# Key-value sums in quarters of the array, queries' A and B in halves, and the first weight slice loaded between the two pieces of the first batch's values

## The chip, the cores and the metric

One core of one Trainium2 chip runs the whole program. The metric is device time in microseconds (us), from the first to the last instruction of one execution, as the median of three executions. Engines are named as in the profile: PE (TensorE matmuls), PEld (its weight loads), DVE (VectorE), ACT (ScalarE), POOL (GpSimd), SP (SyncE, which issues nearly all DMAs).

## The reference, cut to what matters

An attention without softmax feeds a gated linear unit. `phi` is the outer product of two small projections of a vector of 32 numbers, so it has 64 features.

```python
batch, n_heads, seq, head_dim = (4, 4, 1088, 32);  r = 8
def phi(x):
    a = einsum('rd,bhsd->bhsr', S1, x)          # "A"
    b = einsum('rd,bhsd->bhsr', S2, x)          # "B"
    return einsum('bhsi,bhsj->bhsij', a, b)     # 64 features
kv  = einsum('bhsf,bhsd->bhfd', phi(k), v);  z = sum(phi(k), axis=2)
x   = einsum('bhsf,bhfd->bhsd', phi(q), kv) / (einsum('bhsf,bhf->bhs', phi(q), z) + 1e-6)
# n_tokens 4352, d_model 128, d_ff 1536
xn  = x / sqrt(mean(x*x) + 1e-6) * rms_g
out = (silu(xn @ w_gate) * (xn @ w_val)) @ w_out
```

## The kernel before, in words

The 4352 tokens are cut into nine chunks (eight of 512, one of 256). For each batch of keys (`kside`), PE makes A and B (line 489), DVE or POOL the outer product `phi` (L511), and PE the sums over tokens `kv`. For batch 0 these sums are 36 matmuls of 64 x 34 (L541: nine tiles of tokens by four heads); two heads share a group of 64 output rows each. For the first two chunks of queries, `qphi` makes A and B with the tokens as the stationary side (L582, 128 tokens a matmul), the outer product `phn` on DVE (L591), four transposes (L601, which write `phiq` through a copy, L615). From chunk 2 on it takes A and B to DRAM (`far`, L631), reads them back spread over partitions (`at` L638, `bt` L645) and multiplies them on POOL or DVE (L651). `qside` then multiplies `phiq` by `kv` (`nmm`, L669), divides (L727, L728, L720), takes the mean square (L734, L744), its root on POOL (L765), scales (`xn`, L768 on DVE or L788 on ACT), transposes (L772), and splits the result into `x_hi` (L795, ACT) and `x_lo` (L775, DVE).

The weights come as 64-bit words in twelve slices (`weights(j)`, L391). Each is turned into f32 by an Abs on ACT or DVE (L338 or L318 first), then L318, L323, L328 and L332 on DVE, and then split into `w_hi` (L243, ACT, or L244, DVE) and `w_lo` (L250, POOL, or L251, DVE). A slot (chunk c, slice j) is a gate and a value product of three matmuls each (L830), a Silu on ACT (L837), the product `h` on DVE (L841) and the output matmuls (L848 in f32 for the first twelve slots, later L861 with `h_hi`, L243, and `h_lo`, L250 or L251). Chunks 0 and 1 go through slices 0 to 5 first, then through 6 to 11.

Nothing of the order is written out by hand: every step is a task with a cost, a key and its ways (which engine may do it, with a penalty), and `Plan.run` lists them greedily by these. The order it finds is then fixed, one queue for each engine, and an instruction that waits holds up all that stands behind it on its engine. PE is kept busy in gaps by `keep_warm`, matmuls of zeros (L300). The numbers at the head of the file are such penalties and keys; DMAs are issued by SP in the order that the plan finds.

Of the kernel before, what the change touches and what calls it, by code (L numbers as in the profile page):

```python
# [21 lines left out]
F = R * R  # L22
NT = B * S
P = 128
# [3 lines left out]
KT = 9  # L28
SP = KT * P
HALF = 64  # L30
# [28 lines left out]
HOP = 160  # L59
COPY_DVE = 600  # L60
REST_DVE = 500
ABS_ACT = -300
NATURAL = 2
PHIS = 2
PUT_DVE = 100
PHIQ_DVE = 600
CUT = 6
TURNED = (1, 2, 3)
HBUFS = 3
GAIN = -28.5  # L70
EXACT = 2
EARLY = 12
SPLIT = 6
HEAD = 2
K1 = -41,9,10,-28.2
VT1 = (-15, -14, -13)
SBD = (1,)
AB2 = (-21, -20, -19)
KVO = ()
Q0 = (-61, -57, -56)  # L80
LATER = 12
KLATE = 2500
DLAT = 2400
CHAIN = -52
WAIT = 150
WKEY = {0: -50, 1: -43}
XN_ACT = 150
Q0L = -97.8
Q1 = (8, 6, 5)
Q1L = -25  # L90
KO = (20, 18, 16)
QO = (20, 10, 6)


class Buf:
# [115 lines left out]
def attention_then_glu(ctx, tc, kT, v, qT, sw, w, gain, out):  # L211
    nc = tc.nc
# [9 lines left out]
    def ps(name, bufs):  # L222
        return plan.buf(psum, [P, 512], F32, name, bufs)

    def pe(ns, key, emit, reads, writes, part=False):
        plan.add({"pe": (ns, emit, 0, part)}, key, reads, writes)
# [52 lines left out]
    for b in range(B):  # L279
        t = const.tile([P, 2, 2 * (D + 1)], F32, name=f"kv{b}")  # L280
# [6 lines left out]
    sblk_t = const.tile([P, NB], F32, name="s_t")  # L287
# [99 lines left out]
    def weights(j, key, early):  # L387
        raw, tmp = sb("w_raw", [P, 3 * P, 2], RAWS, U32), sb("w_tmp", [P, 3 * P], TBUFS)
        load(
            P * 3 * P * 8, early,  # L390
            lambda: nc.sync.dma_start(  # L391
                out=raw().rearrange("p n c -> p (n c)"), in_=w.bitcast(U32)[:, 6 * P * j:6 * P * (j + 1)]
            ), [raw],
        )
        to_f32(3 * P, key, lambda: w_f[:, j].rearrange("p a n -> p (a n)"), raw, tmp, [raw], [tmp], [("w", j)])
        split(j, slice(0, 2), key)

    abs_of, ahead = {}, {}
# [65 lines left out]
    def kside(b, keys, early):  # L464
        first = b == 0
        kab, kphi, key = keys
        kt, vt, kv = sb("kt", [P, SP], 2), sb("vt", [P, KT, H, VA], 2), kvs[b]
# [11 lines left out]
        piece = [next(g for g, (_, e) in enumerate(pieces) if hi <= e) for _, hi in groups]  # L479
        abs_ = [sb("ab", [P, 2, 3, H, R], 3) for _ in groups]  # L480
        phis = [sb("phi", [P, 3, H * F], 4) for _ in groups]
# [20 lines left out]
        for i, (lo, hi) in enumerate(groups):  # L502
            g, m, ts = piece[i], hi - lo, slice(0, hi - lo)
            ab_ps, o = (banks[i], 0) if first else (banks[i // 2], i % 2 * 3 * HALF)
# [30 lines left out]
        for i, (lo, hi) in enumerate(groups):  # L535
            def kvmm(lo=lo, hi=hi, phi=phis[i]):
                kvv = acc()[:, :2 * VA].rearrange("p (a x) -> p a x", x=VA)
                for t in range(lo, hi):
                    for h in range(H):
                        rows = slice((h % 2) * F, (h % 2 + 1) * F)  # L540
                        nc.tensor.matmul(  # L541
                            out=kvv[rows, h // 2, :], lhsT=phi()[:, t - lo, h * F:(h + 1) * F], rhs=vt()[:, t, h, :],
                            start=(t == 0 and h < 2), stop=(t == KT - 1), skip_group_check=True,
                        )

            pe(275 * (hi - lo), key, kvmm, [(phis[i], i), (vt, piece[i])], [acc], True)
        for hh in range(2):
            def put(eng, rows=slice(hh * F, (hh + 1) * F), xs=slice(hh * (D + 1), (hh + 1) * (D + 1))):
                kvv = acc()[:, :2 * VA].rearrange("p (a x) -> p a x", x=VA)
# [15 lines left out]
    def qphi(c, kab):  # L565
        n = CHUNKS[c]
        nt = n // P
        first = c == 0
        key0 = kab
        q, phi = phiqs[c]  # L570
        if c < NATURAL:

            ab, pn = sb("abq", [P, 4, H, R], 1), sb("phn", [P, 4, H * F], 1)
            for u in range(0, nt, 2):
                kab = key0 + (1 if first and u else 0)
                us = slice(u, u + 2)
                ab_ps = ps("att", 3)
                tr = ps(("g_ps", "v_ps")[u // 2], 2) if first else ps("att", 3)

                def abmm(u=u, ab_ps=ab_ps):  # L580
                    for t in range(2):
                        nc.tensor.matmul(  # L582
                            out=ab_ps()[:, t * HALF:(t + 1) * HALF], lhsT=q()[:, (u + t) * P:(u + t + 1) * P], rhs=sblk_t,
                            start=True, stop=True,
                        )

                def near(ab_ps=ab_ps):
                    return ab_ps()[:, :2 * HALF].rearrange("p (th c r) -> p th c r", c=2, r=R)

                def outer(us=us, near=near):  # L590
                    nc.vector.tensor_tensor(  # L591
                        out=pn()[:, us].rearrange("p t (h i j) -> p (t h) i j", h=H, i=R),
                        in0=near()[:, :, 0, :].unsqueeze(3).to_broadcast([P, 2 * H, R, R]),
                        in1=ab()[:, us].rearrange("p t h r -> p (t h) r").unsqueeze(2).to_broadcast([P, 2 * H, R, R]),
                        op=ALU.mult,
                    )

                def turn(u=u, tr=tr):
                    for p in range(2):
                        for t in range(2):  # L600
                            nc.tensor.transpose(  # L601
                                out=tr()[:, (2 * p + t) * P:(2 * p + t + 1) * P], in_=pn()[:, u + t, p * P:(p + 1) * P], identity=ident
                            )

                pe(440, kab, abmm, [q, "sblk"], [ab_ps])
                act(
                    HALF, kab, lambda us=us, near=near: nc.scalar.copy(
                        out=ab()[:, us].rearrange("p t h r -> p (t h) r"), in_=near()[:, :, 1, :]
                    ), [ab_ps], [(ab, u)],
                )  # L610
                dve(2 * 268, kab, outer, [(ab, u), ab_ps], [(pn, u)])
                pe(440, kab, turn, [(pn, u)], [tr])

                def put(eng, u=u, tr=tr):
                    eng(out=phi()[:, :, u * P:(u + 2) * P], in_=tr().rearrange("p (a s) -> p a s", a=2))  # L615

                plan.add({
                    "act": (512 * 0.835 + 144, lambda put=put: put(nc.scalar.copy), 0),
                    "dve": (512 * 1.04 + 140, lambda put=put: put(nc.vector.tensor_copy), PUT_DVE),
                }, kab, [tr], [(phi, u)])  # L620
        else:


            m = n // 2
            ab, at, bt = sb("abt", [P, 256], 2), sb("at", [P, 2, 512], 1), sb("bt", [P, 2, 512], 1)
            ab_ps = abs_of[c]
            act(m, kab, lambda: nc.scalar.copy(out=ab()[:, :m], in_=ab_ps()[:, :m]), [ab_ps], [ab])
            far = plan.buf(dram, [2 * H * R, 512], F32, "far", 2)
            for t in range(2):
                load(  # L630
                    H * R * n * 4, kab, lambda t=t: nc.sync.dma_start(  # L631
                        out=far()[:, t * m:(t + 1) * m], in_=ab()[t * HALF:(t + 1) * HALF, :m]
                    ), [(far, t)], [ab],
                )
            for p in range(2):
                rows = slice(2 * p * R, 2 * (p + 1) * R)
                load(
                    P * n * 8, kab, lambda p=p, rows=rows: nc.sync.dma_start(  # L638
                        out=at()[:, p, :n], in_=far()[rows, :n].unsqueeze(1).to_broadcast([2 * R, R, n])
                    ), [(at, p)], [(far, 0), (far, 1)],  # L640
                )
                for o in range(2):
                    rows = slice((H + 2 * p + o) * R, (H + 2 * p + o + 1) * R)
                    load(
                        F * n * 8, kab, lambda p=p, o=o, rows=rows: nc.sync.dma_start(  # L645
                            out=bt()[o * F:(o + 1) * F, p, :n], in_=far()[rows, :n].unsqueeze(0).to_broadcast([R, R, n])
                        ), [(bt, p, o)], [(far, 0), (far, 1)],
                    )

                def times(eng, p=p):  # L650
                    eng.tensor_tensor(out=phi()[:, p, :n], in0=at()[:, p, :n], in1=bt()[:, p, :n], op=ALU.mult)  # L651

                plan.add({
                    "pool": (n * 2.1 + 150, lambda times=times: times(nc.gpsimd), 0),
                    "dve": (n * 1.04 + 140, lambda times=times: times(nc.vector), PHIQ_DVE, True),
                }, kab, [(at, p), (bt, p, 0), (bt, p, 1)], [(phi, "p", p)])
# [35 lines left out]
    def qside(c, keys, also=None):  # L692
# [3 lines left out]
        phi = phiqs[c][1]  # L696
# [58 lines left out]
        for u, wd in ((0, 2), (2, 2)) if first else ((0, nt),):  # L755
# [2 lines left out]
            xt = ps("att", 3)  # L758
            if first and not u:

                ahead[1] = [ps("att", 3) for _ in range(2)]
            ids = list(range(u, u + wd, 2))

            def root(us=us):
# [137 lines left out]
    qphi(0, Q0[0])  # L902
    qside(0, Q0[1:])
    for j in range(NJ):
        weights(j, WKEY.get(j, slots.index((0, j)) - 4), -30 + 2 * j)
    for j in range(NJ):
        split(j, slice(2, 3), max(EARLY, slots.index((0, j))) + j % CUT - SPLIT if (0, j) in slots else 0)
    t1 = begin[1]
# [72 lines left out]
```

## Time and profile before

| | |
|---|---|
| median of 3 executions | 266.39 us (266.28 to 266.45) |
| profiled execution, its own time | 267.68 us |
| its span, first to last instruction | 265.9 us |
| PE busy | 260.0 us, 98% |
| DVE, ACT, POOL busy | 189.6, 153.0, 66.8 us |
| DMA | 22.11 MB, 83 GB/s over the span |

Busy time is time in which an engine has an instruction in it; the clock that PE was granted is shown in tenths of full speed. A row of a timeline has the start, the duration, the engine, the line and the tiles (out<-in), the shape, how many instructions it merges, and in brackets how long the engine sat idle before it and what ended that. A f32 matmul that is no transpose leaves two records, so "x48" at L541 are 24 matmuls.

### The profile page before, as it was taken

The page shows a single profiled execution, that of the slowest core. Times are in us where ns is not written, and L with a number is a line of the kernel's source. Part 1 is how long each engine was busy: PE and PEld are TensorE (multiplying, and loading weights), DVE is VectorE, ACT ScalarE, POOL GpSimd, SP SyncE. Part 2 cuts the span into 40 slices and gives each one's busy share as a digit, 9 for nine tenths or more (in the row PEclk, how much of TensorE's full clock was granted, in tenths as well). Part 3 has the DMA queues.
Part 4 walks back from the last instruction along what each step waited for, and adds up shares of the span by engine and source line. Part 5 has one row for each costly group of instructions (what it writes and reads, how often), then busy time and mean ns, then how long its engine had stood idle before and what let it go on. Part 6 is the DMA issues. An engine that isn't in the chain of part 4 may idle for free.

```text
span 265.9 us, 5111 instructions
## 1 busy us (share of the span) xinstructions
PE 260.0 (98%) x1913; PEld 206.8 (78%) x1913; DVE 189.6 (71%) x375; ACT 153.0 (58%) x319; POOL 66.8 (25%) x83
## 2 busy tenths in 40 slices
PE   8989999999989999999999999999999999999995
PEld 6877676678867887878887877788878888788894
DVE  3789997787956886677566796677667566766532
ACT  4377673484744644565556554665656565665662
POOL 5053661265060150002700220012200700100262
PEclk9999999999999999999999999999999999999999
DMA  6999801721511430035002500034002100100010
GB/s 201 362 382 313 264 2 32 218 64 62 148 49 53 125 85 2 1 101 145 13 2 79 140 20 4 0 101 118 1 0 76 55 0 0 42 1 0 0 42 21
DMA packets 13097, 22.11 MB, mean 83 GB/s; under 512 B 1680, under 2 KB 5904, under 8 KB 13072
## 3 DMA queue, kind: packets, MB, share of 16 engines
q1 hardware_dynamic: 12928, 21.72, 26.4%
q8 instruction: 15, 0.25, 0.4%
q14 instruction: 10, 0.08, 0.1%
q10 hardware_dynamic: 144, 0.07, 0.1%
HBM read 18.69 MB, written 3.08 MB: 82 GB/s over the span
## 4 chain that ended last, share of the span: by engine, by line
PE 84%; DMA 8%; SPq 3%; POOL 1%; ACT 1%; issue 1%; DVE 1%; POOLq 0%
PE g_ps L830 25%; PE v_ps L830 25%; PE o_ps L861 21%; DMA w_raw<-w 4%; PE o_ps L848 4%; PE att L669 3%; DMA bt<-far 2%; DMA far<-abt 2%; PE att L414 1%; PE att L685 1%; PE att L772 1%; PE att L489 1%; SPq L645 1%; POOL h_lo L250 1%; POOL phiq L651 0%
## 5 line engine op out<-in xcount | busy, mean ns | idle before, releaser
L841 DVE TENSOR_TENSOR h<-v_ps,s 128x512 f32<-128x512 f32 (+2 forms) x109 | 71.1, 655 | 25.1 <-PE v_ps L830 13.7
L243 ACT CAST h_hi<-h 128x512 fp32r<-128x512 f32 (+1 forms) x91 | 54.2, 596 | 49.2 <-DVE h L841 49.0
L837 ACT ACTIVATE s<-g_ps 128x512 f32<-128x512 f32 (+1 forms) x108 | 62.1, 575 | 25.1 <-PE g_ps L830 22.5
L251 DVE TENSOR_TENSOR h_lo<-h,h_hi 128x512 fp32r<-128x512 f32 x76 | 53.3, 704 | 32.2 <-ACT h_hi L243 31.1
L830 PE MATMUL g_ps<-x_hi,w_hi 128*128 128x512 f32 (+1 forms) x110 | 45.8, 416 | 0.0
L830 PE MATMUL v_ps<-x_hi,w_hi 128*128 128x512 f32 (+1 forms) x110 | 42.0, 382 | 0.0
L830 PE MATMUL g_ps<-x_hi,w_lo 128*128 128x512 f32 (+1 forms) x110 | 41.9, 381 | 0.0
L830 PE MATMUL v_ps<-x_hi,w_lo 128*128 128x512 f32 (+1 forms) x110 | 41.6, 378 | 0.0
L830 PE MATMUL v_ps<-x_lo,w_hi 128*128 128x512 f32 (+1 forms) x110 | 41.5, 378 | 0.0
L830 PE MATMUL g_ps<-x_lo,w_hi 128*128 128x512 f32 (+1 forms) x110 | 41.5, 378 | 0.0
L861 PE MATMUL o_ps<-h_lo,w_hi 128*128 128x512 f32 (+1 forms) x94 | 36.0, 383 | 0.9 <-POOL h_lo L250 0.9
L765 POOL TENSOR_TENSOR rstd<-ms,mhalf 128x4 f32<-128x4 f32 (+1 forms) x10 | 9.2, 924 | 108.8 <-DVE ms L781 108.3
L861 PE MATMUL o_ps<-h_hi,w_lo 128*128 128x512 f32 (+1 forms) x94 | 36.1, 384 | 0.0
L861 PE MATMUL o_ps<-h_hi,w_hi 128*128 128x512 f32 (+1 forms) x94 | 35.9, 382 | 0.0
L830 PEld LDWEIGHTS g_ps<-x_hi,w_hi 128*128 128x128 f32 x110 | 20.7, 188 | 6.3 <-issue 1.5
L651 POOL TENSOR_TENSOR phiq<-at,bt 128x512 f32<-128x512 f32 (+1 forms) x14 | 18.0, 1285 | 29.3 <-DMA bt<-far 22.1
L250 POOL TENSOR_TENSOR h_lo<-h,h_hi 128x256 fp32r<-128x256 f32 (+1 forms) x18 | 18.2, 1018 | 27.4 <-ACT h_hi L243 27.3
L830 PEld LDWEIGHTS v_ps<-x_hi,w_hi 128*128 128x128 f32 x110 | 20.7, 188 | 4.8 <-DVE h L841 0.5
L830 PEld LDWEIGHTS g_ps<-x_hi,w_lo 128*128 128x128 f32 x110 | 20.7, 188 | 4.8 <-issue 1.2
L250 POOL TENSOR_TENSOR w_lo<-w_f,w_hi 128x256 fp32r<-128x256 f32 (+1 forms) x24 | 17.8, 755 | 26.3 <-ACT w_hi L243 26.2
L830 PEld LDWEIGHTS g_ps<-x_lo,w_hi 128*128 128x128 f32 x110 | 20.8, 189 | 4.2
L830 PEld LDWEIGHTS v_ps<-x_lo,w_hi 128*128 128x128 f32 x110 | 20.7, 188 | 4.1
(107 smaller groups left out, 302.7 us busy)
## 6 DMA issues: line engine op xcount, KB each, us to landing
w_raw<-w SPq DMA_DIRECT2D x12, 384.0 KB
at<-far SPq DMA_DIRECT2D x12, 256.0 KB
bt<-far SPq DMA_DIRECT2D x24, 128.0 KB
q<-qT SPq DMA_DIRECT2D x8, 256.0 KB
outT<-o_sb SPq DMA_DIRECT2D x8, 256.0 KB
vt<-v SPq DMA_DIRECT2D x9, 204.0 KB
kt<-kT SPq DMA_DIRECT2D x9, 192.0 KB
far<-abt SPq DMA_DIRECT2D x12, 64.0 KB
```

The costliest lines, as they stand in the source:

```text
L243: "act": (n * 0.835 + 172, lambda: nc.scalar.copy(out=out(), in_=in_()), 0),
L250: "pool": (n * 2.1 + 150, lambda: nc.gpsimd.tensor_tensor(out=out(), in0=in_(), in1=hi(), op=ALU.subtract), 0),
L251: "dve": (n * 1.04 + 140, lambda: nc.vector.tensor_tensor(out=out(), in0=in_(), in1=hi(), op=ALU.subtract), penalty, True),
L414: nc.tensor.matmul(out=acc()[rows, :F], lhsT=vt()[:, t, h, :D], rhs=phis[t // 3]()[:, t % 3, h * F:(h + 1) * F], start=(t == 0), stop=(t = ...
L651: eng.tensor_tensor(out=phi()[:, p, :n], in0=at()[:, p, :n], in1=bt()[:, p, :n], op=ALU.mult)
L669: nc.tensor.matmul(out=nv[hf * HALF:(hf + 1) * HALF, t, p, :], lhsT=phiqs[c][1]()[:, p, l0:l0 + HALF], rhs=kvs[(STARTS[c] + l0) // S][:, p ...
L765: nc.gpsimd.tensor_tensor(out=rstd()[:, us, 0], in0=ms()[:, us], in1=mhalf[:, us], op=ALU.pow)
L830: nc.tensor.matmul(out=acc()[:, cs], lhsT=wt[:, j, i3, :], rhs=x()[:, cs], start=(i == 0), stop=(i == 2))
L837: act(n, t + 0.3, lambda: nc.scalar.activation(out=s()[:, :n], in_=gps()[:, :n], func=AF.Silu), cols(gps, whole[0]), [s])
L841: lambda cs=cs: nc.vector.tensor_tensor(out=h()[:, cs], in0=vps()[:, cs], in1=s()[:, cs], op=ALU.mult),
L848: lambda cs=cs: nc.tensor.matmul(out=o_ps()[:, cs], lhsT=w_f[:, j, 2], rhs=h()[:, cs], start=first, stop=last and cs.stop == n),
L861: nc.tensor.matmul(out=o_ps()[:, :n], lhsT=wt[:, j, 2, :], rhs=x()[:, :n], start=first and i == 0, stop=last and i == 2,)
```

## The change

Three edits in the code, and new values for the plan's numbers. The sums of batch 0 (L541) are made by 72 matmuls of 32 x 34 instead of 36 of 64 x 34, and the plan is told 130 ns a tile of tokens instead of 275. A and B of the first two chunks' queries (L582) are made by matmuls of 64 tokens, twice as many, which the plan counts among the forms that use a part of the array. The first weight slice has a load key of its own, `W0L`, that lies between those of the two pieces of the first batch's values. The A and B of batch 1's keys write to banks of `g_ps` and `v_ps` instead of `att`. The other numbers move penalties (an outer product `phiq` on DVE costs 300 more than on POOL instead of 600; the copy of the transposes on DVE 600 instead of 100; Abs on DVE 500 instead of 300; `xn` on ACT nothing instead of 150) and keys; three slots instead of two go in halves (`HEAD`).

```diff
-ABS_ACT = -300
+ABS_ACT = -500
-PUT_DVE = 100
-PHIQ_DVE = 600
+PUT_DVE = 600
+PHIQ_DVE = 300
-SPLIT = 6
-HEAD = 2
-K1 = -41,9,10,-28.2
+SPLIT = 8
+HEAD = 3
+K1 = (-45, 3, 15, -29.5)
-AB2 = (-21, -20, -19)
+AB2 = (4, -20, 4)
-CHAIN = -52
-WAIT = 150
+CHAIN = -47
+WAIT = 100
-XN_ACT = 150
+XN_ACT = 0
+W0L = -97.3
...
                     for h in range(H):
-                        rows = slice((h % 2) * F, (h % 2 + 1) * F)
-                        nc.tensor.matmul(
-                            out=kvv[rows, h // 2, :], lhsT=phi()[:, t - lo, h * F:(h + 1) * F], rhs=vt()[:, t, h, :],
-                            start=(t == 0 and h < 2), stop=(t == KT - 1), skip_group_check=True,
-                        )
-
-            pe(275 * (hi - lo), key, kvmm, [(phis[i], i), (vt, piece[i])], [acc], True)
+                        for x in range(0, F, F // 2):
+                            r0 = h % 2 * F + x
+                            nc.tensor.matmul(
+                                out=kvv[r0:r0 + F // 2, h // 2, :], lhsT=phi()[:, t - lo, h * F + x:h * F + x + F // 2],
+                                rhs=vt()[:, t, h, :], start=(t == 0 and h < 2), stop=(t == KT - 1), skip_group_check=True,
+                            )
+
+            pe(130 * (hi - lo), key, kvmm, [(phis[i], i), (vt, piece[i])], [acc], True)
...
                     for t in range(2):
-                        nc.tensor.matmul(
-                            out=ab_ps()[:, t * HALF:(t + 1) * HALF], lhsT=q()[:, (u + t) * P:(u + t + 1) * P], rhs=sblk_t,
-                            start=True, stop=True,
-                        )
+                        for hf in range(2):
+                            s0 = (u + t) * P + hf * HALF
+                            nc.tensor.matmul(
+                                out=ab_ps()[hf * HALF:(hf + 1) * HALF, t * HALF:(t + 1) * HALF], lhsT=q()[:, s0:s0 + HALF],
+                                rhs=sblk_t, start=True, stop=True,
+                            )
...
-                ahead[1] = [ps("att", 3) for _ in range(2)]
+                ahead[1] = [ps(name, 2) for name in ("g_ps", "v_ps")]
...
-        weights(j, WKEY.get(j, slots.index((0, j)) - 4), -30 + 2 * j)
+        weights(j, WKEY.get(j, slots.index((0, j)) - 4), W0L if j == 0 else -30 + 2 * j)
```

What the plan makes of it, at three places. Lines of the changed kernel stand up to five higher than before (L489 is L490, L541 is L544, L582 is L587, L601 is L606, L651 is L656, L669 is L674, L772 is L777, L830 is L835, L841 is L846).

SP, the first loads. `kt`, `vt` and `q` are the keys, values and queries, `w_raw` a weight slice. Before:

```order
L472 DMA kt<-kT 128x512
L472 DMA kt<-kT 128x640
L562 DMA q<-qT 128x512
L475 DMA vt<-v 128x544
L475 DMA vt<-v 128x680
L391 DMA w_raw<-w 128x768
L899 DMA gain_t<-gain 128x1
L472 DMA kt<-kT 128x384 x3
```

and now:

```order
L473 DMA kt<-kT 128x512
L473 DMA kt<-kT 128x640
L565 DMA q<-qT 128x512
L476 DMA vt<-v 128x544
L392 DMA w_raw<-w 128x768
L476 DMA vt<-v 128x680
L473 DMA kt<-kT 128x384 x3
L904 DMA gain_t<-gain 128x1
```

The first weight slice stands ahead of the second piece of the values; the rest of this piece is the same.

PE, from the sums of batch 0 to the first gate matmul of chunk 0. `phn` and `xn` are transposed, `kv_83` is batch 0's sums. Before:

```order
L582 MATMUL att<-s_t,q 128x64 x4
L541 MATMUL o_ps<-vt,phi 64x34 x24
L601 MATMUL g_ps<-ident,phn 128x128 x4
L541 MATMUL o_ps<-vt,phi 64x34 x12
L601 MATMUL v_ps<-ident,phn 128x128 x4
L669 MATMUL att<-kv_83,phiq 64x66 x16
L300 MATMUL att<-const-float32-0.0 1x128 x11
L772 MATMUL att<-ident,xn 128x128 x2
L489 MATMUL att<-s_t,kt 64x64 x18
L772 MATMUL att<-ident,xn 128x128 x2
L830 MATMUL g_ps<-x_hi,w_hi 128x256
```

and now:

```order
L587 MATMUL att<-s_t,q 64x64 x8
L544 MATMUL o_ps<-vt,phi 32x34 x32
L606 MATMUL g_ps<-ident,phn 128x128 x4
L301 MATMUL att<-const-float32-0.0 1x128
L544 MATMUL o_ps<-vt,phi 32x34 x40
L606 MATMUL v_ps<-ident,phn 128x128 x4
L674 MATMUL att<-kv_83,phiq 64x66 x16
L490 MATMUL g_ps<-s_t,kt 64x64 x12
L490 MATMUL v_ps<-s_t,kt 64x64 x6
L777 MATMUL att<-ident,xn 128x128 x2
L301 MATMUL att<-const-float32-0.0 1x128 x2
L835 MATMUL g_ps<-x_hi,w_hi 128x256
```

Batch 1's A and B (18 matmuls) moved ahead of the first transposes, the eleven matmuls of zeros became three, and the second pair of transposes went behind the gate products.

DVE, after chunk 0's sum of its two output parts (`o_sb`). `phiq` is the outer product of a later chunk's queries, `h` and `h_lo` belong to slots. Before:

```order
L892 TENSOR_TENSOR o_sb<-o_ps,part 128x512
L841 TENSOR_TENSOR h<-v_ps,s 128x512
L775 SCALAR_TENSOR_TENSOR x_lo<-att,gain_t,x_hi 128x512
L841 TENSOR_TENSOR h<-v_ps,s 128x512
L251 TENSOR_TENSOR h_lo<-h,h_hi 128x512 x2
L841 TENSOR_TENSOR h<-v_ps,s 128x512 x2
L251 TENSOR_TENSOR h_lo<-h,h_hi 128x512
```

and now:

```order
L897 TENSOR_TENSOR o_sb<-o_ps,part 128x512
L846 TENSOR_TENSOR h<-v_ps,s 128x512
L780 SCALAR_TENSOR_TENSOR x_lo<-att,gain_t,x_hi 128x512
L846 TENSOR_TENSOR h<-v_ps,s 128x512
L656 TENSOR_TENSOR phiq<-at,bt 128x512
L252 TENSOR_TENSOR h_lo<-h,h_hi 128x512 x2
L846 TENSOR_TENSOR h<-v_ps,s 128x512 x2
L656 TENSOR_TENSOR phiq<-at,bt 128x512
L252 TENSOR_TENSOR h_lo<-h,h_hi 128x512 x2
```

Both `phiq` products of this chunk stand on DVE now. Of the fourteen in all, fourteen stood on POOL before; now eight stand on DVE and six on POOL.

## Rows read from the trace of the kernel before

**Rows 1.** The page: busy time of the engines, and two lines of the span in 40 equal slices (busy tenths of PE, and the clock granted to it).

```profile
PE 260.0 (98%) x1913; PEld 206.8 (78%) x1913; DVE 189.6 (71%) x375; ACT 153.0 (58%) x319; POOL 66.8 (25%) x83
...
PE   8989999999989999999999999999999999999995
...
PEclk9999999999999999999999999999999999999999
```

**Rows 2.** Waits of PE within the program: the line that waited, what it waited for, us in total, times, the longest.

```profile
PE o_ps L861 <- POOL h_lo L250: 0.9, 1, 0.9
PE att L772 <- DVE xn L768: 0.8, 1, 0.8
...
PE o_ps L848 <- DVE h L841: 0.2, 1, 0.2
```

**Rows 3.** Timeline of PE, 7 to 19 us.

```profile
7.66 1.67 PE L541 MATMUL o_ps<-vt,phi 128*64 128x34 f32 x48
...
9.85 0.89 PE L541 MATMUL o_ps<-vt,phi 128*64 128x34 f32 x24
10.68 0.65 PE L601 MATMUL v_ps<-ident,phn 128*128 128x128 f32 x4
11.38 1.32 PE L669 MATMUL att<-kv,phiq 128*64 128x66 f32 x32
12.62 2.60 PE L300 MATMUL att<-const-float32-0.0 128*1 128x128 f32 x22
16.04 0.41 PE L772 MATMUL att<-ident,xn 128*128 128x128 f32 x2 [0.81 <-DVE xn L768]
16.38 1.27 PE L489 MATMUL att<-s_t,kt 128*64 128x64 f32 x36
17.63 0.52 PE L772 MATMUL att<-ident,xn 128*128 128x128 f32 x2
17.90 0.36 PE L830 MATMUL g_ps<-x_hi,w_hi 128*128 128x256 f32 x1
...
18.22 0.29 PE L830 MATMUL g_ps<-x_lo,w_hi 128*128 128x256 f32 x1
18.34 0.56 PE L582 MATMUL att<-s_t,q 128*128 128x64 f32 x4
18.71 0.36 PE L830 MATMUL v_ps<-x_hi,w_hi 128*128 128x256 f32 x1
```

**Rows 4.** Timeline of DVE between the copy of the first transposes and the first `x_lo`.

```profile
11.35 0.36 DVE L323 TENSOR_SCALAR w_tmp<-w_tmp 128x384 uint32<-128x384 uint32 x1
...
12.34 0.56 DVE L332 SCALAR_TENSOR_TENSOR w_f<-w_raw,w_tmp 128x384 uint32<-128x384 uint32 x1
12.93 0.17 DVE L727 TENSOR_SCALAR den<-att 128x8 f32<-128x8 f32 x1
...
15.47 0.42 DVE L768 TENSOR_TENSOR xn<-x,rstd 128x256 f32<-128x256 f32 x1
...
16.99 0.49 DVE L775 SCALAR_TENSOR_TENSOR x_lo<-att,gain_t,x_hi 128x256 fp32r<-128x256 f32 x1 [0.52 <-ACT x_hi L795]
```

**Rows 5.** Timelines of SP (the issue that waited for `vt`'s first piece, and the one that waited for its second), and of ACT (the first work on slice 0, which waited for its load).

```profile
7.54 0.33 SPq L391 DMA_DIRECT2D w_raw<-w  x1
...
8.56 0.33 SPq L562 DMA_DIRECT2D q<-qT  x1
...
9.52 0.55 ACT L338 ACTIVATE w_tmp<-w_raw 128x384 f32<-128x384 f32 x1 [1.71 <-DMA w_raw<-w]
```

**Rows 6.** Timeline of PE at the sums of batch 1: matmuls of 32 columns of the array with 32 (L410) and 64 (L414) moving columns, and the one behind them.

```profile
43.29 0.34 PE L410 MATMUL att<-ab 128*32 128x32 f32 x17
43.44 0.26 PE L414 MATMUL att<-phi,vt 128*32 128x64 f32 x3
...
44.60 0.66 PE L685 MATMUL att<-q,sab 128*64 128x128 f32 x8
```

**Rows 7.** Timelines of ACT and POOL near the first gate: `x_hi`, the `xn` of the second half of the chunk, and the root before it.

```profile
16.48 0.47 ACT L795 ACTIVATE x_hi<-att,gain_t 128x256 fp32r<-128x256 f32 x1 [0.47 <-PE att L772]
17.07 0.70 ACT L788 ACTIVATE xn<-x,rstd 128x128 f32<-128x128 f32 x2
...
16.30 0.74 POOL L765 TENSOR_TENSOR rstd<-ms,mhalf 128x2 f32<-128x2 f32 x1 [0.99 <-DVE ms L781]
```

**Rows 8.** Timelines of POOL, SP and PE at chunk 3's queries: the two products of `phiq` and the `h_lo` behind them; the two stores to `far` and the loads behind them; the PE matmul that waited.

```profile
73.25 1.29 POOL L651 TENSOR_TENSOR phiq<-at,bt 128x512 f32<-128x512 f32 x1 [6.50 <-PE v_ps L830]
75.72 1.30 POOL L651 TENSOR_TENSOR phiq<-at,bt 128x512 f32<-128x512 f32 x1 [1.17 <-DMA bt<-far]
76.98 1.74 POOL L250 TENSOR_TENSOR h_lo<-h,h_hi 128x512 fp32r<-128x512 f32 x1
...
61.97 1.14 SPq L631 DMA_DIRECT2D far<-abt  x2
...
66.92 0.56 SPq L638 DMA_DIRECT2D at<-far  x1
...
78.77 0.51 PE L861 MATMUL o_ps<-h_lo,w_hi 128*128 128x512 f32 x1 [0.85 <-POOL h_lo L250]
```

**Rows 9.** DVE there, and what POOL's `phiq` products waited for over the whole span (us, times).

```profile
71.27 0.69 DVE L841 TENSOR_TENSOR h<-v_ps,s 128x512 f32<-128x512 f32 x1
...
  DMA bt<-far: 22.1, 9
```

More of the change, by code (lines that the diff above doesn't have):

```diff
@@ L83 @@
 DLAT = 2400
-CHAIN = -52
-WAIT = 150
+CHAIN = -47
+WAIT = 100
 WKEY = {0: -50, 1: -43}
-XN_ACT = 150
+XN_ACT = 0
 Q0L = -97.8
-Q1 = (8, 6, 5)
-Q1L = -25
+Q1 = (8, 5, 4)
+Q1L = -23
+W0L = -97.3
 KO = (20, 18, 16)
-QO = (20, 10, 6)
+QO = (18, 10, 7)
 class Buf:
@@ L603, in turn @@
                             )
-                pe(440, kab, abmm, [q, "sblk"], [ab_ps])
+                pe(250, kab, abmm, [q, "sblk"], [ab_ps], True)
                 act(
```

## The prediction, made blind

> **What bounds the kernel now.** I read the page first: PE is busy 98% of a span of 265.9 us, no other engine over 78%, and its granted clock is full in every slice [rows 1]. So the time is PE's, and the list of PE's waits shows what of it is not work: 0.8 us for `xn` near the start, 0.2 and 0.9 later [rows 2]. Third, PE's timeline: between the last product with batch 0's sums and the first transposes of `xn` stand 2.60 us of matmuls of zeros and the wait of 0.81, which is 3.4 us from 12.62 to 16.04 in which PE computes nothing; from 16.04 on it works without a break worth naming except at 22.6 and 78.77 [rows 2, 3, 8]. Hence only three things can shorten the span: the first gate product coming earlier than 17.90, the wait at 78.77 going away, or PE getting less to do after 17.90. DVE's timeline says why the gap is there: the denominators of the first two token tiles could be read when the first half of the L669 matmuls is done, at 11.38 + 0.62 = 12.00, but `den` starts at 12.93, right behind the conversion of weight slice 0, which DVE finishes at 12.90 [rows 3, 4]. That conversion begins when the slice lands, at about 9.5; the two pieces of the values land at about 7.54 and 8.56, where SP's waits for them end [rows 5].
>
> **The change, part by part.** All times are those of the profiled execution. Its own time is 267.68 us, 1.8 over its span, and the median of the runs is 266.39; I carry a difference in the span over to the median one to one.
>
> *Loads.* Slice 0 and the second piece of the values change places. The slice took 0.95 us of the queue (8.56 to 9.5), the piece 1.02 (7.54 to 8.56) [rows 5]: now the slice is there at 8.5 and the values at 9.5. Slice 0 gains 1.0 us, the sums of batch 0 must wait 1.0 us longer for their second piece.
>
> *Sums in quarters.* The last twelve matmuls of L541 took from 9.85 to 10.68, 69 ns each [rows 3]; 36 of them are 2.5 us. The new form, 32 columns of the array with 34 moving, isn't in this trace. From below: nine matmuls of L410 with 32 moving columns took from 43.29 to 43.44, 17 ns each; from above 36 of L414 with 64 took from 43.44 to 44.60, 32 ns each [rows 6]. By columns 34 lies next to the first, I take 20 (72 in 1.4 us; bounds 1.2 and 2.3). [...]
>
> On the path 40 of the 72 stand behind the values' landing: start at 9.6 (as 7.66 follows 7.54 [rows 3, 5]), 0.8 us, end at 10.4 instead of 10.68 (bounds 10.3 and 10.9). So the better matmuls just pay for the later load, with 0.3 us over.
>
> *The way to the first gate.* The L669 matmuls began 0.70 us after the sums' end; now that is 11.1, and their first half is done at 11.7 [rows 3]. Slice 0's conversion ended at 12.90 [rows 4]; 1.0 earlier is 11.9, and DVE loses a copy of the transposes and one of the sums to ACT but gets a cast. I let `den` start at 11.8, 1.1 us earlier. From `den` to the start of `xn` were 2.54 us [rows 4]; `xn` is on ACT now, 0.70 [rows 7] for 0.42, but isn't behind a weight operation: its end moves from 15.89 to 14.9. From there to the end of `x_lo` (17.48) were 1.59 us [rows 4]; ACT now has the second half's squares in that stretch, for which I add 0.1: `x_lo` is done at 16.6, and the third gate matmul, which stood at 18.22 [rows 3], starts there, 1.6 us earlier. Batch 1's A and B (16.38 to 17.63 [rows 3]) cost nothing, since they lie in the old gap; were their keys late they would push the gate, by up to 1.25. The second pair of transposes (17.63 to 17.90) is still to come: net gain there 1.3 us.
>
> *What PE then lacks.* PE runs ahead of its supply. The second half of `x` needs squares, root (0.74), `xn` (0.70, among weight casts on ACT), transposes, `x_hi` (0.47) and `x_lo` (0.49) [rows 4, 7], each a little over 0.1 from the next: about 3 us after the first `xn` at 14.9 plus what ACT and POOL do in between, so 18.5 to 19.0. Until then PE has four groups of three matmuls (0.36 each [rows 3]) and one AB of 0.3, some 1.8 us from 16.6 on: 0.1 to 0.6 short. Slice 1's `w_lo` waits behind the root on POOL, and chunk 1's `phn` and `phiq` copies come up earlier, too. I charge 0.8 us for these waits (bounds 0.3 and 1.3). The head gains 0.5 us (bounds 0 and 1.0).
>
> *Halves for A and B.* Two matmuls of L582 took 0.37 us (18.34 to 18.71); four of 64 at L489's rate of 69 ns (18 from 16.38 to 17.63) are 0.28 [rows 3]. Twice 0.09, less a change of form: nothing, with 0.2 as the bound. The pair at the start is hidden behind the values' first piece. The third slot in halves is the same columns: nothing, bound 0.2 either way.
>
> *The wait at 78.77.* PE stood 0.85 us for an `h_lo` on POOL, which started at 76.98 behind two `phiq` products that had waited for `bt` [rows 8]. Both products go to DVE, so that `h_lo` isn't behind them: 0.85 gained, if DVE finds its operands there.
>
> Sum: 0.5 + 0.85 = 1.35 us off. 266.39 - 1.35 = 265.0.
>
> **The rivals.** *The wait at chunk 3 moves to DVE.* DVE gets to its first `phiq` after the `h` of 71.27, at 71.96 [rows 9]; POOL's could start at 73.25 [rows 8]. With the same transfers DVE stands 1.3 us, and two `h_lo` and all later `h` stand behind it. For it: the far store took from 61.97 to beyond 66.9 there [rows 8], and nothing in the change shortens that. Against: the transfer's delay belongs to that moment, and DVE had air around it. PE then pays about what it paid, 0.85: 265.9.
>
> *DVE's waits for transfers, at several chunks: slower.* Eight of the fourteen products stand on DVE now. On POOL nine of them waited 22.1 us in total for `bt` [rows 9], 2.5 us each, and it cost PE little, since POOL is busy 25%; DVE is busy 71% [rows 1] and makes every `h`. At 0.85 us a place it takes three places to outweigh the gain and make the kernel measurably slower: 265.0 + 2.55 = 267.6. Against: the products stand later in DVE's queue than POOL's did.
>
> [...]
>
> *No waits after the first gate.* If PE's supply keeps up, the head gains 1.2: 264.3. *No gain in the head*, if the values land later than the swap says: 265.5.
>
> **How the numbers follow.** Forecast 0.48 (its own range 264.4 to 265.6), wait moved to DVE 0.20, several DVE waits 0.12, dear quarters 0.04, no waits after the gate 0.10, no gain in the head 0.06. A measurement can tell about 0.2%, 0.53 us: below 265.86 is faster, above 266.92 slower. Faster: 0.45 of the forecast's 0.48, 0.08 of the second, both last cases but 0.01: 0.68. Slower: 0.09 of the DVE waits, 0.04 and 0.01: 0.14. Same: 0.18. The range 264.0 to 266.8 leaves out some 0.03 below and 0.13 above.
>
> **What would show it.** Slice 0's Abs starts near 8.6; L544's second part starts near 9.6 and takes 0.8 us; `den` stands near 11.8; the first gate's third matmul near 16.6; PE's list of waits gets several of 0.1 to 0.6 us before 24; the wait for POOL's `h_lo` is gone. It is wrong if DVE's idle time is put down to `bt`, if L544 takes over 30 ns a matmul, or if PE, with no zeros to work on, is granted half the clock somewhere before 20 us.

## The result: slower, and the profile after

The changed kernel takes 268.56 us (median of 4, 267.94 to 269.12) against 266.40 for the kernel before: a ratio of 1.0081, 95% interval 1.0055 to 1.0108. Measured again beside other kernels it took 268.67 (6 executions) against 266.90, a ratio of 1.0068 (1.0044 to 1.0093). I had forecast 265.0, faster, with a range up to 266.8. The sign was wrong, and the time lies above the range.

The page of the changed kernel, which answers to [rows 1]: busy times, and the two lines of the span in 40 slices.

```profile
PE 258.3 (97%) x1991; PEld 205.5 (77%) x1991; DVE 192.4 (72%) x377; ACT 155.8 (58%) x330; POOL 55.7 (21%) x77
...
PE   8589999999999999999999999999999999999995
...
PEclk9979999999999999999999999999999999999999
...
q8 instruction: 15, 0.25, 0.4%
```

The last line is a DMA queue: packets, MB, share of the 16 engines. Two digits say where to look: in the second slice (6.7 to 13.4 us) PE is busy half of the time, and in the third (13.4 to 20.0) it was granted 0.7 of its clock. Everything behind looks as before. The list of PE's waits answers to [rows 2] (line that waited, on what, us in total, times, longest):

```profile
PE att L674 <- issue: 2.4, 1, 2.4
PE o_ps L544 <- DMA vt<-v: 0.8, 2, 0.5
...
PE att L777 <- ACT xn L793: 0.7, 1, 0.7
PE g_ps L835 <- DVE x_lo L780: 0.4, 1, 0.4
```

The `h_lo` of POOL is gone from it, as I had said; the kernel before, profiled again, lacks it too (see "The wait at 78.77"). In its place stands a wait of 2.4 us that the profile puts down to "issue", that is, to nothing it can see. PE's timeline around it answers to [rows 3]:

```profile
9.52 0.90 PE L544 MATMUL o_ps<-vt,phi 128*32 128x34 f32 x80 [0.47 <-DMA vt<-v]
10.35 0.66 PE L606 MATMUL v_ps<-ident,phn 128*128 128x128 f32 x4
13.38 2.03 PE L674 MATMUL att<-kv,phiq 128*64 128x66 f32 x32 [2.37 <-issue]
15.19 1.47 PE L490 MATMUL g_ps<-s_t,kt 128*64 128x64 f32 x24
16.47 0.54 PE L490 MATMUL v_ps<-s_t,kt 128*64 128x64 f32 x12
17.66 0.62 PE L777 MATMUL att<-ident,xn 128*128 128x128 f32 x2 [0.65 <-ACT xn L793]
...
19.41 0.39 PE L835 MATMUL g_ps<-x_lo,w_hi 128*128 128x256 f32 x1
```

L674 stands at 13.38, where I had it at 11.1. Its last operand was there long before: ACT's copy of `phiq` is this row, done at 11.63, and `kv` was done at 10.94.

```profile
11.04 0.59 ACT L620 COPY phiq<-v_ps 128x512 f32<-128x512 f32 x1
```

What PE did then it did slowly: the 32 records of L674 took 1.8 us, 1.2 before [rows 3]. The same span by stretches (length, PE busy and its instructions, granted clock, DMA share, GB/s) shows a clock of 0.5 right behind the 2.1 us in which PE had nothing to do:

```profile
11.00:13.10 2.10, 0.01 (x1) 1.00 1.03 402
13.10:16.50 3.40, 3.12 (x58) 0.50 1.04 414
16.50:20.00 3.50, 2.75 (x29) 1.00 0.52 170
```

So the third gate product came at 19.41 and not at 18.22 [rows 3], 1.2 us later instead of 1.6 earlier.

### The profile page after: what moved, and what is told of

The parts are those of the page before. It is cut to its first block, busy times and chain, and to the rows that moved or that the text cites. A ratio compares the mean times of both kernels' runs of the same rounds, so it can differ in the third digit from the quotient of the medians.

```text
span 267.2 us, 5268 instructions
## 1 busy us (share of the span) xinstructions
PE 258.3 (97%) x1991; PEld 205.5 (77%) x1991; DVE 192.4 (72%) x377; ACT 155.8 (58%) x330; POOL 55.7 (21%) x77
## 4 chain that ended last, share of the span: by engine, by line
PE 88%; DVE 4%; DMA 2%; ACT 2%; issue 1%; SPq 1%; POOL 0%; DVEq 0%
PE g_ps L835 26%; PE v_ps L835 26%; PE o_ps L866 23%; PE o_ps L853 4%; PE att L674 3%; DMA vt<-v 2%; PE att L777 1%; PE att L690 1%; PE att L490 1%; PE att L415 1%; DVE phi L512 1%; DVE w_tmp L319 1%; DVE phn L596 0%; DVE w_f L333 0%; ACT phiq L620 0%
## 5 line engine op out<-in xcount | busy, mean ns | idle before, releaser
L846 DVE TENSOR_TENSOR h<-v_ps,s 128x512 f32<-128x512 f32 (+2 forms) x109 | 71.0, 654 | 25.4 <-PE v_ps L835 14.6
L835 PE MATMUL g_ps<-x_hi,w_hi 128*128 128x512 f32 (+1 forms) x111 | 47.2, 425 | 0.1
L835 PE MATMUL g_ps<-x_lo,w_hi 128*128 128x512 f32 (+1 forms) x111 | 41.8, 377 | 0.4 <-DVE x_lo L780 0.4
L835 PE MATMUL v_ps<-x_hi,w_hi 128*128 128x512 f32 (+1 forms) x111 | 42.0, 378 | 0.1
L835 PE MATMUL v_ps<-x_lo,w_hi 128*128 128x512 f32 (+1 forms) x111 | 41.8, 376 | 0.0
L835 PE MATMUL g_ps<-x_hi,w_lo 128*128 128x512 f32 (+1 forms) x111 | 41.7, 376 | 0.0
L835 PE MATMUL v_ps<-x_hi,w_lo 128*128 128x512 f32 (+1 forms) x111 | 41.5, 374 | 0.0
L251 POOL TENSOR_TENSOR h_lo<-h,h_hi 128x512 fp32r<-128x512 f32 (+1 forms) x20 | 20.6, 1034 | 64.5 <-ACT h_hi L244 64.5
L835 PEld LDWEIGHTS g_ps<-x_hi,w_hi 128*128 128x128 f32 x111 | 20.9, 188 | 7.2 <-issue 1.7
L835 PEld LDWEIGHTS g_ps<-x_hi,w_lo 128*128 128x128 f32 x111 | 20.9, 188 | 5.8 <-issue 1.7
L835 PEld LDWEIGHTS g_ps<-x_lo,w_hi 128*128 128x128 f32 x111 | 20.9, 188 | 4.9 <-DVE x_lo L780 0.9
L835 PEld LDWEIGHTS v_ps<-x_hi,w_hi 128*128 128x128 f32 x111 | 20.8, 188 | 4.4 <-DVE h L846 0.2
L835 PEld LDWEIGHTS v_ps<-x_lo,w_hi 128*128 128x128 f32 x111 | 20.8, 188 | 4.0
L835 PEld LDWEIGHTS v_ps<-x_hi,w_lo 128*128 128x128 f32 x111 | 20.9, 188 | 4.0
L251 POOL TENSOR_TENSOR w_lo<-w_f,w_hi 128x128 fp32r<-128x128 f32 (+1 forms) x24 | 15.5, 664 | 25.4 <-ACT w_hi L244 21.0
```

The costliest lines, as they stand in the source:

```text
L251: "pool": (n * 2.1 + 150, lambda: nc.gpsimd.tensor_tensor(out=out(), in0=in_(), in1=hi(), op=ALU.subtract), 0),
L835: nc.tensor.matmul(out=acc()[:, cs], lhsT=wt[:, j, i3, :], rhs=x()[:, cs], start=(i == 0), stop=(i == 2))
L846: lambda cs=cs: nc.vector.tensor_tensor(out=h()[:, cs], in0=vps()[:, cs], in1=s()[:, cs], op=ALU.mult),
```

## The experiments

**Theories.** A: PE had no code. The page has a queue 8 of the kind "instruction", fifteen transfers of 16 KB, which I take for PE's code, and the trace has the first of them in this span at 11.09 us, just after PE fell silent. The quarters put 144 instructions more ahead of L674 (36 more matmuls, each two records of PE and two weight loads), and the halves of A and B another 16. B: the wait belongs to the new order (the swapped loads, the copies on ACT, the new banks), and the profile merely fails to name it.

**The code, with the order kept.** Three kernels change nothing but how many matmuls make the same sums (and, in one, the same A and B); the plan's numbers stay, so the steps in every queue stay.

`a_halves`: the changed kernel with 36 matmuls again.

```diff
-                        for x in range(0, F, F // 2):
-                            r0 = h % 2 * F + x
-                            nc.tensor.matmul(out=kvv[r0:r0 + F // 2, h // 2, :], ...
+                        rows = slice((h % 2) * F, (h % 2 + 1) * F)
+                        nc.tensor.matmul(out=kvv[rows, h // 2, :], ...
```

> The changed kernel in its own order, with batch 0's sums made by 36 matmuls of 64 x 34 again; the plan's numbers stay, so every queue holds the same steps. Theory A (PE ran out of code: it had the instructions up to the first L674 product, the 449th of its stream, and the next 16 KB of them landed only at about 13.3 us): 144 instructions fewer stand ahead of L674, so the end of the loaded code moves behind batch 1's A and B. No wait of L674 put down to issue, full clock between 13 and 17 us, L674 near 12.2 (the sums behind the load take 1.4 us instead of 0.8), third gate product near 17.4 instead of 19.41, time 266.5 (266.0 to 267.0). Theory B (the wait belongs to the new order: the swapped loads, the copy of phiq on ACT or the banks): the wait of about 2 us stays and the time is 268.6 or more.

Measured: 266.17 us (10 executions), ratio to before 0.9959 (0.9935 to 0.9984); once more, beside others, 266.44 and 0.9988 (0.9970 to 1.0005), for which this was on record:

> The version with halves once more, beside the three others: 266.2 (265.8 to 266.5), 0.4 to 0.6 under the kernel before.

No wait for issue, clock 1.00 throughout:

```profile
11.62 1.36 PE L673 MATMUL att<-kv,phiq 128*64 128x66 f32 x32
12.82 0.87 PE L490 MATMUL g_ps<-s_t,kt 128*64 128x64 f32 x24
...
16.91 0.39 PE L834 MATMUL g_ps<-x_lo,w_hi 128*128 128x256 f32 x1
```

`a_mixed`: quarters for the five tiles behind the load alone, and the first chunk's A and B whole.

```diff
+                        W = F if t < 4 else F // 2
-                        for x in range(0, F, F // 2):
+                        for x in range(0, F, W):
...
+                        wide = P if c == 0 else HALF
-                        for hf in range(2):
+                        for s0 in range(0, P, wide):
```

> The changed kernel in its own order, with quarters only for the five token tiles behind the load of the values' second piece, halves for the four ahead of it, and the first chunk's A and B by matmuls of 128 tokens again. Theory A (PE ran out of code): 80 instructions fewer ahead of L674, so the end of the loaded code lies in batch 1's A and B, reached at about 13.1: a wait of at most 0.4 us there, full clock, L674 near 11.8, third gate product near 17.0, time 266.0 (265.5 to 266.7). Theory B (the new order): as the changed kernel, 268.6.

Measured: 266.67 us, ratio 0.9989 (0.9971 to 1.0008). The wait is there, in another place, and three times as long as I had expected:

```profile
11.07 1.37 PE L675 MATMUL att<-kv,phiq 128*64 128x66 f32 x32
12.28 0.40 PE L490 MATMUL g_ps<-s_t,kt 128*64 128x64 f32 x8
13.87 0.69 PE L490 MATMUL g_ps<-s_t,kt 128*64 128x64 f32 x16 [1.19 <-issue]
```

`b_quarters`: the kernel before, its own order and loads, with 72 matmuls for the sums.

```diff
+                        for x in range(0, F, F // 2):
+                            r0 = h % 2 * F + x
+                            nc.tensor.matmul(out=kvv[r0:r0 + F // 2, h // 2, :], ...
-                        nc.tensor.matmul(out=kvv[rows, h // 2, :], ...
             pe(275 * (hi - lo), key, kvmm, [(phis[i], i), (vt, piece[i])], [acc], True)
```

> The kernel before in its own order and with its own numbers; only batch 0's sums are made by 72 matmuls of 32 x 34. Theory A (PE ran out of code): L669 begins at the 431st instruction of PE's stream, so PE stops some five products into it, near 11.5, until the next code lands between 12.5 and 13.5; den moves from 12.93 to between 13.7 and 14.8, PE's waits show 1 to 2 us put down to issue, and the time is 267.0 to 268.5. Theory B (the wait belongs to the new order): nothing of it here, 266.2 to 266.4.

Measured: 269.20 us (10 executions, 267.47 to 270.50), ratio 1.0077 (1.0044 to 1.0109). One edit alone makes the kernel before as slow as the changed one. The time lies above the 267.0 to 268.5 that I expected under theory A, by the clock's share (below); the place of the stop and its length are as expected. PE stops five products into L670:

```profile
11.40 0.56 PE L670 MATMUL att<-kv,phiq 128*64 128x66 f32 x10 [0.16 <-DVE kv L551]
13.78 0.92 PE L670 MATMUL att<-kv,phiq 128*64 128x66 f32 x22 [1.81 <-issue]
```

That settles it for A. The count makes it exact. Summing the matmul records of PE's timeline up to the wait gives 222 in the changed kernel (16 of zeros, 36, 16, 64, 4, 2, 80, 4), 222 in `a_mixed` (… 32, and 8 of L490), and 222 in `b_quarters` (… 10 of L670): PE stops behind the same number of instructions whatever line stands there. In every kernel that stopped, it went on 2.3 to 2.5 us after the first transfer on queue 8 had begun: 11.09 and 13.37 in the changed kernel, 11.53 and 13.87 in `a_mixed`, 11.44 and 13.78 in `b_quarters`; three more kernels below stop behind 222 records, too. The kernel before got its transfer no earlier (11.96), but reaches its 222nd record only at 17.13, inside the L489 that starts at 16.38 [rows 3], 2.8 us after the code was there by the same lag (11.96 + 2.4): it had slack that no list of waits shows. `a_halves` reaches it at 15.71.

The later transfers are met by no such wait. The fifteen of 16 KB began 234 of PE's recorded instructions (matmuls and weight loads) apart on average in the changed kernel and 244 in the one before, though single distances go from 113 to 371; PE's list in the changed kernel has one wait for issue, 2.4 us at the first of them, and none at the fourteen others. The last 234 recorded instructions ahead of that stop took PE 3.0 us (7.7 to 10.7), where the transfers begin 16.7 us apart on average (11.1 to 244.7).

**The clock's share.** The ten executions of `b_quarters` sort by their granted clock: with 0.998 or 0.999 they took 267.5 to 268.1 us, with 0.992 to 0.994 they took 269.0 to 269.6, with 0.987 they took 270.2 and 270.5. One stretch of 3.4 us at half the clock leaves 0.994 over such a span (1.7 lost of 267). So in this kernel the stop alone is worth about 1 us over the 266.77 of the kernel before in this series, and each such stretch another 1.0 to 1.5. A stretch can also cost nothing: in `a_mixed` three executions with 0.994 took 266.6 to 267.0 us, the seven others 266.0 to 267.1. Where the stretch lies in an execution that wasn't profiled isn't known.

The stretch comes with the stop in most executions: all ten of the changed kernel and seven of ten of `b_quarters` have a clock of 0.994 or less, one of twenty of `a_halves`, and two of the 79 of the kernel before that were run beside these kernels. In the changed kernel one such stretch is in the profile above. From the start of L674 to the third gate product it took 6.03 us, in `a_halves` 5.29 (11.62 to 16.91): 0.74 us of the clock's cost were on the path. Two kernels below bear this out: `a_raws2`, which stopped and ran there at half the clock, took 6.05, and `a_light`, which stopped and kept its clock until 18.58, took 5.35.

`after2` is the changed kernel once more, with no edit.

> The changed kernel once more, beside the two others: 268.6 (267.9 to 269.5), a wait of L674 for issue of 1.5 to 2.5 us, and times that go with the granted clock of the execution.

Measured: 268.67 us (268.04 to 269.57); the profiled one, 269.39, waited 3.4 us for issue, longer than I expected: its first transfer began at 12.13, and it went on at 14.54. The wait follows the transfer, and this kernel's times spread over 1.5 us, where the first ten of `a_halves` spread over 0.6. They go with the granted clock only loosely: 268.0 and 268.8 at 0.994, 269.6 at 0.991, but 268.4, 268.5 and 269.4 at 0.987.

**Why does the code come so late?** Two kernels take loads out of the stretch ahead of 11 us.

`a_raws2`:

```diff
-RAWS, TBUFS = 7, 2
+RAWS, TBUFS = 2, 2
```

> The changed kernel with two buffers for raw weight slices instead of seven; quarters everywhere. PE's, DVE's and ACT's orders are the changed kernel's up to the first gate; on SP only one slice is issued behind batch 1's keys instead of three, so that two slices of 0.95 us each no longer stand in the queue when PE's next code is asked for. If the code comes late because it is transferred beside and behind these loads, its transfer starts 1 to 2 us earlier than 11.09, L674's wait for issue shrinks from 2.4 to between 0.4 and 1.4 us, and the time is 266.3 to 267.6 (later slices land later, which may cost some of it). Rival: the delay has nothing to do with the loads; the transfer starts at 11.0 or later, the wait stays over 2 us, the time 268.5.

Measured: 273.94 us, ratio 1.0288 (1.0258 to 1.0319). The first transfer began at 10.53, half a microsecond earlier, and L674 stood at 12.86:

```profile
12.86 2.03 PE L674 MATMUL att<-kv,phiq 128*64 128x66 f32 x32 [1.90 <-ACT w_tmp L339]
```

The profile puts this wait, and the one of `a_light` below, down to ACT's conversion of a later weight slice, which L674 doesn't read; PE stopped behind its 222nd record again. Neither expectation holds: the transfer moved less than 1 us, and the wait of 1.9 lies between the two. A wait of PE for a `w_hi`, 1.5 us, is new; the later slices have other costs further on, which I haven't followed and had put too low.

`a_light`:

```diff
+        n = P if j in (1, 2, 3) else 6 * P
...
+            if n < 6 * P:
+                nc.gpsimd.memset(to[:, n:], 0)
+            nc.sync.dma_start(out=to[:, :n], in_=w.bitcast(U32)[:, 6 * P * j:6 * P * j + n])
```

> The changed kernel, quarters everywhere, with slices 1 to 3 loaded to a sixth (64 KB each instead of 384) and zeros for the rest of them, so the weights of these slices are left out in part; PE's, DVE's and ACT's orders are the changed kernel's, POOL gets three fillings of 128 x 640. The instructions ahead of L674 are the same 448. If PE's code comes late because these loads stand in the same queues, its first transfer starts before 9.5 instead of at 11.09, PE has the code by 10.9 and waits for it under 0.5 us, clock full, third gate product before 17.2, time 264.5 to 267. If the delay has nothing to do with the loads, the transfer starts at 10.5 or later, L674 waits 1.5 us or more for issue, and the time is 268 or more.

Measured: 268.81 us, ratio 1.0073 (1.0045 to 1.0100). The transfer began at 10.39 and L679 (the old L674) at 12.67, still 1.7 us late:

```profile
12.67 1.16 PE L679 MATMUL att<-kv,phiq 128*64 128x66 f32 x32 [1.72 <-ACT w_tmp L339]
```

The wait and the time are those of the second expectation, the transfer lies between the two, just ahead of 10.5: other loads moved up into the room, so that some 340 to 400 GB/s went on until 10.3, and the first transfer moved up by 0.7 to 1.7 us against the two profiles of the changed kernel. Whether these loads are what delays the code stays open. Against it: in `b_again`, the kernel before once more, the loads fell to between 81 and 197 GB/s from 8.0 to 9.0 us, and the transfer still began only at 12.26. What the runs show is that its first transfer begins between 10.4 and 12.3 us in all fourteen profiles, with 230 to 444 of PE's recorded instructions begun by then, and earliest in the two with fewer loads ahead of it.

**A version that keeps some of both.** `a_part` is `a_mixed` with quarters for the last two tiles only.

```diff
-                        W = F if t < 4 else F // 2
+                        W = F if t < 7 else F // 2
```

> The changed kernel in its own order, with quarters for the last two token tiles alone, halves for the seven ahead, and the first chunk's A and B by matmuls of 128 tokens: the 449th instruction of PE's stream lies two or three matmuls before the end of batch 1's A and B. Theory A: no wait for code over 0.4 us, none that holds ACT's copies ahead of xn; L674 near 11.4, third gate product near 16.7 (16.91 with halves everywhere), time 266.0 (265.7 to 266.5), 0.1 to 0.2 under that of halves everywhere. Theory B: a wait of 1 us or more wherever L674 or L490 stands, 267 or more.

Measured: 265.88 us (7 executions), ratio 0.9968 (0.9950 to 0.9987), and with five rounds:

> The version with quarters for the last two tiles alone, once more: 265.9 (265.7 to 266.3), 0.6 to 0.9 under the kernel before and 2.5 to 3 under the changed one.

Measured: 266.17 us (12 executions) against 266.90, ratio 0.9978 (0.9955 to 1.0000). It is under the kernel before by 0.2 to 0.3%, with a second interval that touches 1, and under the changed one by about 2.6 us. From `a_halves` (0.9959 and 0.9988) it can't be told, so that quarters are not shown to bring anything over halves even where next to no time is lost for code. In the first profile PE still stops, again behind 222 records, but so late that little is lost (0.59 us, where I expected 0.4 at most), since the transposes would have waited for `xn` anyway:

```profile
13.08 0.40 PE L490 MATMUL v_ps<-s_t,kt 128*64 128x64 f32 x8
14.07 0.34 PE L490 MATMUL v_ps<-s_t,kt 128*64 128x64 f32 x4 [0.59 <-issue]
14.65 0.62 PE L778 MATMUL att<-ident,xn 128*128 128x128 f32 x2 [0.24 <-ACT xn L794]
...
16.51 0.39 PE L836 MATMUL g_ps<-x_lo,w_hi 128*128 128x256 f32 x1
```

In the second profile PE doesn't stop (the transfer began at 11.46, the 222nd record came at 13.79), waits 1.0 us for `xn` instead, and has its third gate product at 17.03; that product scatters by half a microsecond between two executions of one kernel.

**The wait at 78.77.** `b_again` is the kernel before without an edit.

> The kernel before once more. Its profiled execution was 267.68 us where the median was 266.39. If the 0.85 us of PE at 78.77 belongs to every execution, this profile shows it again. If it belongs to that execution alone, PE's list lacks it here, the span is near 264.7, and the 0.85 that I took off the sum was never in the median.

Measured: 266.64 us (10 executions); the profiled one has a span of 264.8, 1.1 under the one of [rows 1]. PE's list of waits, PE's third gate product, and POOL and PE at the place of [rows 8]:

```profile
PE att L772 <- DVE xn L768: 0.8, 1, 0.8
...
PE o_ps L848 <- DVE h L841: 0.2, 1, 0.2
...
18.05 0.28 PE L830 MATMUL g_ps<-x_lo,w_hi 128*128 128x256 f32 x1
...
75.03 1.29 POOL L651 TENSOR_TENSOR phiq<-at,bt 128x512 f32<-128x512 f32 x1 [0.68 <-DMA bt<-far]
76.27 1.32 POOL L250 TENSOR_TENSOR h_lo<-h,h_hi 128x512 fp32r<-128x512 f32 x1
...
77.64 0.50 PE L861 MATMUL o_ps<-h_lo,w_hi 128*128 128x512 f32 x1
```

The `h_lo` ran 1.32 us where it had taken 1.74, behind products that waited less for `bt`, and PE waits 0.1 instead of 0.85. `a_h_phiq` is `a_halves` with all fourteen `phiq` on POOL:

```diff
-PHIQ_DVE = 300
+PHIQ_DVE = 600
```

> The version with halves (changed kernel, 36 matmuls for the sums) with the penalty of phiq on DVE at 600 again: all fourteen phiq products stand on POOL, and the steps around them from chunk 2 on are planned anew; the head is the same. If the move to DVE brought the 0.85 us of the wait at 78.77, this is 0.85 slower than the version with halves. If that wait isn't in ordinary executions, it is the same within 0.3. If DVE's waits for bt cost anything, it is faster.

Measured: 266.37 us against the 266.44 of `a_halves` in the same series. The move is worth nothing that can be seen. In the changed kernel the two products stand on DVE, one of them 0.30 us idle for `bt`, and nobody waits:

```profile
74.61 0.69 DVE L656 TENSOR_TENSOR phiq<-at,bt 128x512 f32<-128x512 f32 x1 [0.30 <-DMA bt<-far]
...
77.68 0.68 DVE L656 TENSOR_TENSOR phiq<-at,bt 128x512 f32<-128x512 f32 x1
```

**The swap of the loads.** `a_h_w0l` is `a_halves` with

```diff
-W0L = -97.3
+W0L = -30
```

> The version with halves with the load of slice 0 back behind the second piece of the values (W0L = -30); the plan then puts slice 0's conversion on DVE behind den and x of the first two tiles. If the swap of the loads carries the head's gain, the first gate product moves back by 0.5 to 1.0 us from 16.28 and the time is 266.7 to 267.3. If the gain came from the other numbers (batch 1's A and B in the gap, xn on ACT), the sums behind the values' second piece end near 10.6, the first gate product stays between 15.8 and 16.6, and the time is 266.0 to 266.6.

Measured: 267.68 us (5 executions), ratio 1.0035 (1.0022 to 1.0049). Both expectations were half right: the first gate product stands at 16.02, as in the second, and the time is that of the first. PE waited twice for `xn`, 2.0 us, and then ran at half the clock (granted 0.986 to 0.992 in all five executions):

```profile
PE att L776 <- ACT xn L792: 2.0, 2, 1.3
...
18.80:22.30 3.50, 3.36 (x21) 0.54 0.93 319
...
20.26 0.42 PE L834 MATMUL g_ps<-x_hi,w_hi 128*128 128x256 f32 x1
20.47 0.41 PE L834 MATMUL g_ps<-x_hi,w_lo 128*128 128x256 f32 x1
...
22.69 0.28 PE L834 MATMUL v_ps<-x_hi,w_hi 128*128 128x256 f32 x1
22.81 0.28 PE L834 MATMUL v_ps<-x_hi,w_lo 128*128 128x256 f32 x1
```

The rows follow each other by 0.21 us in that stretch and by 0.12 behind it. So `a_halves`, with the swap and the order that the plan makes of it, is 1.2 to 1.5 us faster than without, by this profile not because the first gate comes earlier but because PE isn't left idle around it.

## Why the prediction was wrong, step by step

*Loads: right.* Slice 0's Abs started at 8.65 (8.6 said), the sums' second part at 9.52 (9.6).

*Sums in quarters: the price right, what they bring with them missed.* The 40 matmuls took 9.52 to 10.35, 21 ns each, where I had taken 20 from the nearest rows. The chances hold 0.04 for dear quarters: no run shows a quarter that costs what a half does, 69 ns; these took 21. But I counted time alone. A quarter is as many instructions as a half, so the form doubles their number while each takes a third of its time (21 ns of 69), and PE was at its 222nd record by 10.7, before the transfer of 11.09 had begun. None of the rivals had this: they were about engines and data. This is the step that failed: I let the L669 matmuls (L674 now) start at 11.1, as soon as their data were there, and put PE's supply of code at nothing. They started at 13.38, and the half clock behind the stop took another 0.74, together more than twice the 1.35 that I had forecast as gain.

*The way to the first gate: right where code was there.* In `a_mixed` `den` stands at 11.81 (11.8 said), in `a_part` the third gate product at 16.51 and 17.03 (16.6 said). In the changed kernel `den` came at 14.57 and the product at 19.41, both 2.8 later than said.

*What PE then lacks: right in size.* I charged 0.8. From `b_again` to `a_part` the third gate product came 1.54 earlier (18.05 and 16.51) and the span is 0.8 shorter, so 0.7 were given back, as many as PE's waits of 0.24 for a `w_lo` and 0.43 for an `x_lo` behind it; in `a_part2` it came 1.02 earlier for a span 0.3 shorter, 0.7 again. The head's 0.5 was there for the taking.

*Halves for A and B, the third slot: not shown*; I had put both at nothing, and they weren't tried apart.

*The wait at 78.77: mis-sized against the median.* I saw that the profiled execution was 1.29 us above the median and still carried a wait of that one execution over one to one. In `b_again` the term is 0.1 and not 0.85. Of the sum of 1.35, 0.5 was real.

*The rivals.* Waits of DVE for `bt` didn't come: 2.6 us in three places, none of which PE's list shows. I had named a half clock before 20 us as a sign that I was wrong, but had put it down to PE without zeros to work on; it came at the end of the 2.4 us in which PE stood for issue (0.50 from 13.1 to 16.5). And the rival without waits behind the gate should have read 1.3 and 264.2, by my own net gain.

The sum by the runs, in spans: 264.8 for the kernel before (`b_again`), 0.8 off as in `a_part`, 2.2 on for the stop (L674 at 13.38 and 11.22), 0.74 for the clock: 266.9, where the profile has 267.2. At 159 to 162 us this execution loses some 0.5 that `a_halves` doesn't, which is more than the rest; I haven't followed it.

## What to carry to other kernels

Where an edit multiplies small instructions, count them as well as time them: add up the records on the engine ahead of a wait for issue (222 here, in six kernels) and look up when the transfer on the instruction queue began (10.4 to 12.3 us here). A kernel can be close to such a stop and show nothing of it: 36 matmuls more, 144 instructions, were enough for the kernel before (`b_quarters`, 1.8 us for issue). And a wait that one profiled execution shows is a term against that execution; where its own time lies off the median, see first whether the wait is there twice.

## What the runs showed of the hardware

PE stopped behind its 222nd matmul record (444 recorded instructions with the weight loads) in six kernels here, until 2.3 to 2.5 us after the start of a transfer of 16 KB that took about 1 us. That transfer began between 10.4 and 12.3 us in all fourteen profiles; why no earlier stays open. Waits of PE near the start (2.4 us in the changed kernel, 3.4 in `after2`, 1.3 and 0.7 in `a_h_w0l`) were followed by 3.4 us, or twice that, at half the clock, in some executions of a kernel and not in others: the profiled one of `b_quarters` waited 1.8 us and has a granted clock of 0.998, that of `a_mixed` waited 1.2 and has 1.0. The clock fell from 0.3 us before the end of the last such wait (changed kernel) to 2.5 us behind it (`a_light`, whose waits were 1.7 and 1.2).
